# Attention with soft mixture of experts: the last 64 keys on four quarters of the array, and other positions in the order of tasks

## The chip, the cores and the metric

One core of one Trainium2 chip. The metric is device time of one execution in microseconds (us), the median of several runs; lower is better. The engines are TensorE (PE, its weight loads shown as PEld), VectorE (DVE), ScalarE (ACT), GpSimd (POOL) and SyncE (SP), which issues nearly all DMAs.

## The reference

Two stages. First attention over 8 batches, 8 heads, 576 positions and 64 dimensions, with rotary embedding; then a soft mixture of 8 experts with 4 slots each on its output.

```
q_rot, k_rot = rotate(q), rotate(k)
scores = (1 / sqrt(64)) * q_rot @ k_rot.T
attn = exp(scores - max(scores)); attn /= sum(attn) + 1e-9
x = (attn @ v), heads side by side: 4608 x 512
logits = x @ phi                        # 4608 x 32
d = softmax of logits over the rows;  slot_input = d.T @ x
slot_out = relu(slot_input @ w1[e]) @ w2[e]   # per expert
c = softmax of logits over the slots; out = c @ slot_out
```

## The kernel before

The work goes by pairs of heads: 32 pairs (4 per batch), two heads of a pair on the two halves of the 128 partitions. The 576 keys of a head are four blocks of 128 and a rest of 64; the 576 queries are two halves (n = 0, 1) of 288 columns. For one pair p the tasks are:

- load0, load1 (`fetch`, L136): q and k come in by SP into one of two buffers `x_in`. spin0, spin1 (L141, GpSimd) multiply by cosines and sines, join (L145, VectorE) adds the two parts, high0, high1 (L150, ScalarE) round to 16-bit halves, low (L154, VectorE) forms the remainders; it is the last reader of `x_in`, so it frees the buffer for the load of the pair after next.
- m00 to m31, m_rem (L172, L180, TensorE): 16-bit scores with the queries on the partitions; VectorE takes their maxima (L174, L182), m_min joins them (L186), m_turn, m_half and m_rows bring them as a row into `peak`.
- t00 to t31 (`t_unit`, L228): the scores with keys on the partitions, key block j, half n. Each is four products of 64 rows (high x high, high x low, low x high, and a product that subtracts the maximum) for two heads, which stand on the two row halves of the array and write the two banks of a PSUM buffer. ScalarE takes the exponential (L213) into `a_t`.
- t_rem (L215 to L220): the same for the last 64 keys. Head h reads row half h and writes partitions 64h to 64h + 63, for half n in bank n; first all of n = 0, then all of n = 1. ScalarE's exponential goes to `a_rem` (L220).
- av00 to av41 (L239): the product with v, accumulated in `o_ps` over five steps j. For j = 0 to 3, 128 keys on the rows and 64 columns per head; for j = 4, all 128 rows of `a_rem` (both heads) with a block of v that holds zeros for the other head. o_out (L246, ScalarE) copies the result out; there is one `o_ps`.
- add1, add2, add3 (L255, L257, VectorE) add up the exponentials over the key blocks, total (L269) sums them over the partitions with a matrix of ones and zeros, `pick`, total_out (L274, ScalarE) copies, send (L279 to L281, three DMAs on SP) lays the sums out as `rc`, recip (L287, L288, VectorE) forms 1 / sum, spread (L294) and widen (L301) are DMAs that broadcast it, norm (L304, GpSimd) applies it.
- logits and natural (L353 to L356, L339, L340) feed the second stage. Once per batch, stats hands a list of statistics to step0 to step3, which each work off one entry.

All engines' orders are written out by hand. The table `WHEN` gives each task a position: the fraction modulo 4 is its place in a cycle ("beat"), the quotient says how many pairs ahead or behind it runs. In each of the 32 beats the tasks run through in the order of these places, and each engine's queue follows from it. A beat of TensorE before the change is

```
t00 t01 m20 m21 | av30 av31 av40 av41 | t10 m30 | av00 | t11 m31 | av01 |
m_rem | total | t20 | m_turn | m01 t21 | av10 av11 | logits | t30 m10 m00 |
av20 | t31 m11 | natural | av21 | t_rem
```

where a bar stands where the form of the matmuls (rows x columns of the array that they use) changes. In the same beat VectorE's queue has m20, add3, m21, step0, m30, m31, m_rem, m_min, low, step1, m01, add1, logits_sum, stats, m10, m00, step2, m11, recip, add2, join, step3. SP's queue has widen, load0, load1, send, m_rows, weights, load_v, spread. All scores and small products take their turn in three PSUM buffers `s_ps` of two banks (`bank2`). After the last pair follow the statistics' end, the experts' two layers and the combination.

Of the kernel before, what the change touches and what calls it, by code (L numbers as in the profile page):

```python
# [7 lines left out]
F32 = mybir.dt.float32  # L8
# [7 lines left out]
B, H, S, D = 8, 8, 576, 64  # L16
HALF = D // 2
NP = H // 2
NPAIR = B * NP
DM = H * D  # L20
E, SPE, FF = 8, 4, 1024
NS = E * SPE
# [4 lines left out]
HC = S // 2  # L27
# [16 lines left out]
RC = 12  # L44
PIECE = 4
WHEN = {
    "load0": -15.85, "load1": -15.171, "spin0": -11.45, "spin1": -10.42, "join": -8.349, "high1": -7.786,
    "high0": -6.702, "low": -6.38, "m01": -5.7, "m10": -4.9, "m00": -4.892, "m11": -4.7, "m20": -3.754, "m21": -3.7,
    "m30": -2.9, "m31": -2.7, "m_rem": -2.531, "m_min": -2.49, "m_turn": -1.75, "m_half": -1.74, "m_rows": -1.541,
# [4 lines left out]
    "total_out": 5.55, "send": 5.56, "recip": 7.3, "spread": 7.31, "widen": 8.05, "norm": 9.3, "logits": 10.54,  # L54
    "logits_sum": 10.579, "stats": 10.6, "natural": 11.52, "natural_out": 11.536,
    "sums_turn": 6.0, "sums_wide": 6.3, "norm_wide": 6.4, "logits_late": 7.0, "logits_sum_late": 7.05,
    "natural_late": 7.3, "natural_out_late": 7.35,
    "trickle0": 0.55, "trickle1": 1.55, "trickle2": 2.55, "trickle3": 3.55,
}
QL, QH, KH, KL = range(4)  # L60

# [2 lines left out]
def attn_softmoe(ctx, tc, qk, v, phi, w1, w2, cs, ident, sel, seg, out):  # L64
    nc = tc.nc
    P = 128

    const = ctx.enter_context(tc.tile_pool(name="const", bufs=1))
# [21 lines left out]
    rows = (slice(0, 64), slice(64, P))  # L90
# [11 lines left out]
    peaks = [const.tile([P, S], F16, name=f"peak{i}") for i in range(2)]  # L102
    for t in peaks:
        nc.vector.memset(t, 0.0)
    pick = const.tile([P, 2, NS], F32, name="pick")
    nc.gpsimd.memset(pick, 0.0)
    nc.gpsimd.memset(pick[:, 0, 0:1], 1.0)
    for h in range(2):
        nc.gpsimd.memset(pick[rows[h], 1, h:h + 1], 1.0)

    nc.vector.memset(tiny, 0.0)
    nc.vector.memset(tiny[0:64], 1e-9)
# [14 lines left out]
    half = (slice(0, HC), slice(HC, S))  # L127
# [36 lines left out]
    def bank2():  # L164
        return ps_s.tile([P, 2, 512], F32, name="s_ps")
# [39 lines left out]
    ats = {}  # L205
    rems = {}
# [8 lines left out]
    def t_rem(p):  # L215
        rems[p] = att.tile([P, S], F32, name="a_rem")
        s = bank2()
        for n in range(2):
            score(p, s, slice(512, S), [(rows[h], h, n) for h in range(2)], lambda h, n: n)
        nc.scalar.activation(out=rems[p].rearrange("p (n x) -> p n x", n=2), in_=s[:, :, 0:HC], func=AF.Exp, scale=SCALE)  # L220

    def score(p, s, keys, outs, at):
        hl, pk = halves[p], peaks[p % 2]
        for i, (k, q) in enumerate(((KH, QH), (KH, QL), (KL, QH), (None, None))):
            for o, h, n in outs:
                lhs = lift[rows[h], 0:keys.stop - keys.start] if k is None else hl[rows[h], k, keys]
                rhs = pk[rows[h], half[n]] if k is None else hl[rows[h], q, half[n]]
                nc.tensor.matmul(s[o, at(h, n), 0:HC], lhsT=lhs, rhs=rhs, start=(i == 0), stop=(i == 3))  # L228
# [3 lines left out]
    def av(p, j, n):  # L232
        if j == 0 and n == 0:
            os_[p] = ps_o.tile([P, 2, 512], F32, name="o_ps")
        o, vt = os_[p], vts[p]
        for h in range(2):
            at = P * j + 64 * h
            rhs = ats[p, j][:, h, half[n]] if j < 4 else rems[p][:, half[n]]
            nc.tensor.matmul(o[rows[h], n, 0:HC], lhsT=vt[:, at:at + 64], rhs=rhs, start=(j == 0), stop=(j == 4))  # L239

    xts = {}
    xns = {}
# [21 lines left out]
    def total(p):  # L264
        c, r, a = cts.pop(p), rems[p], ats[p, 3]
        sg[p] = s = bank2()
        for n in range(2):
            for i, (k, m) in enumerate(((0, c[:, 0, half[n]]), (0, c[:, 1, half[n]]), (1, r[:, half[n]]), (0, a[:, 0, half[n]]))):
                nc.tensor.matmul(s[32 * i:32 * i + 32, n, 0:HC], lhsT=pick[:, k, :], rhs=m, start=True, stop=True,  # L269
                                 tile_position=(0, 32 * i))  # L270

    def total_out(p):
# [272 lines left out]
    def fast(task):  # L545
# [15 lines left out]
        "m_half": m_half,  # L561
        "m_rows": lambda p: m_rows(p, nc.sync),
        "t_rem": t_rem,
        "o_out": o_out,
        "add1": lambda p: add(p, 1),
        "add2": lambda p: add(p, 2),
        "add3": lambda p: add(p, 3),
        "total": total,
        "total_out": total_out,
        "send": slow(lambda p: send(p, nc.sync)),  # L570
# [24 lines left out]
    for j in range(5):  # L595
        for n in range(2):
            plan[f"av{j}{n}"] = lambda p, j=j, n=n: av(p, j, n)
# [10 lines left out]
    for t, cc in ((1, 0), (1, 1), (0, 0), (0, 1)):  # L608
        c = half[cc]
# [12 lines left out]
    o = bank2()  # L622
# [53 lines left out]
    p = NPAIR - 1  # L676
# [32 lines left out]
    m, al, dt, xn = state["m"], state["al"], state["dt"], xns.pop(B - 1)  # L709
# [27 lines left out]
    for i in range(NP):  # L737
        nc.tensor.matmul(rp[32 * i:32 * i + 32], lhsT=dn[0:64, P + 32 * i:P + 32 * i + 32],
                         rhs=xn[0:64, 4, i * P:(i + 1) * P], start=True, stop=True, tile_position=(0, 32 * i))
# [37 lines left out]
    def ffn1(grp, f):  # L777
        hp = ps_s.tile([P, 2, 512], F32, name="s_ps")
        for i in range(NP):
            for x in range(4):  # L780
                nc.tensor.matmul(hp[32 * x:32 * x + 32, 0, :], lhsT=st[:, i, SPE * (4 * grp + x):SPE * (4 * grp + x) + 32],  # L781
                                 rhs=w_tiles[16 * grp + 8 * f + 4 * (i // 2) + x][:, i % 2, :],
                                 start=(i == 0), stop=(i == NP - 1), tile_position=(0, 32 * x))
        hs = tail.tile([P, 512], F32, name="hs", bufs=2)
        nc.vector.tensor_scalar_max(out=hs, in0=hp[:, 0, :], scalar1=0.0)
        return hs
# [72 lines left out]
    for grp, f in ((0, 1), (1, 0), (1, 1)):  # L859
        h = ffn1(grp, f)  # L860
# [84 lines left out]
```

## Time and profile before

| | |
|---|---|
| median of 3 runs | 660.27 us (660.04 to 661.91) |
| the profiled execution | 662.53 us, span of its records 660.7 us |
| busy in that span | TensorE 603.1, VectorE 491.5, ScalarE 329.9, GpSimd 309.0 us |
| mean granted TensorE clock | 0.965 of full speed |
| moved by DMA | 102.58 MB |

The profile lists one execution. In a timeline a row gives the start in us, the length, the engine, the line (L228 is line 228 of the kernel), the operation, output <- inputs, and shapes; for matmuls "64*128" is rows x columns of the array. Brackets give idle time of the engine just before, and what ended it. Ends of matmuls are modelled and include the way through the array, so the pace is read from start to start.

### The profile page before, as it was taken

Reading aid. Unit: us, or ns where it says so; the run is one execution under the profiler, and the core shown is the slowest. Engines: PE = TensorE matmul, PEld = TensorE weight load, DVE = VectorE, ACT = ScalarE, POOL = GpSimd, SP = SyncE. Lnnn points to the kernel's source line nnn. Section 1 sums busy time; section 2 is a strip of 40 time slices with the busy share of each in tenths; the row PEclk is TensorE's granted clock in tenths of the full one; section 3 lists DMA queues with packets and bytes.
Section 4 is the critical chain, followed back from the end, with each engine's and each line's share of the span. In section 5 each row is a group of like instructions: output and inputs, shape, how many; then the busy total and the mean of one; then the engine's idle time right before and its main releaser. Section 6 shows DMA issues by size and latency. Waiting matters only on the chain.

```text
span 660.7 us, 15956 instructions
## 1 busy us (share of the span) xinstructions
PE 603.1 (91%) x6480; PEld 311.4 (47%) x6480; DVE 491.5 (74%) x729; ACT 329.9 (50%) x647; POOL 309.0 (47%) x310
## 2 busy tenths in 40 slices
PE   3699999999999999999999999999999999989981
PEld 2344444445444454444444544445444445543550
DVE  5787888898888788887889888988898773332251
ACT  1245555555555556455555555555555545323441
POOL 3683665565565565555635765546556200010000
PEclk9689999999999999999999999999999999859995
DMA  6143444444344444343434443434434135449997
GB/s 233 65 146 111 144 144 143 139 139 147 133 147 140 144 144 144 124 143 133 145 119 142 140 142 120 136 126 142 134 142 144 40 104 172 148 146 321 350 374 261
DMA packets 67746, 102.58 MB, mean 155 GB/s; under 512 B 16216, under 2 KB 43608, under 8 KB 67672
## 3 DMA queue, kind: packets, MB, share of 16 engines
q1 hardware_dynamic: 67658, 101.55, 46.4%
q8 instruction: 51, 0.84, 0.5%
q14 instruction: 23, 0.19, 0.1%
q10 hardware_dynamic: 14, 0.00, 0.0%
HBM read 91.54 MB, written 9.58 MB: 153 GB/s over the span
## 4 chain that ended last, share of the span: by engine, by line
PE 60%; ACT 13%; DVE 11%; issue 7%; DMA 6%; SPq 1%; ACTq 0%; DVEq 0%
PE o_ps L239 23%; PE s_ps L228 16%; ACT a_t L213 6%; DVE nm L174 6%; PE s_ps L172 3%; DMA rc<-s 3%; ACT s L274 3%; PE s_ps L781 2%; PE s_ps L339 2%; PE s_ps L269 2%; PE s_ps L180 2%; ACT a_rem L220 2%; PE s_ps L353 2%; DVE hl L154 1%; DMA w_exp<-in_w 1%
## 5 line engine op out<-in xcount | busy, mean ns | idle before, releaser
L141 POOL TENSOR_TENSOR x_in<-x_in,cs_sb 128x288 f32<-128x288 f32 x248 | 259.1, 1076 | 43.3 <-DMA x_in<-in_qk 41.4
L213 ACT ACTIVATE a_t<-s_ps 128x576 f32<-128x576 f32 x256 | 162.8, 648 | 132.3 <-PE s_ps L228 131.9
L174 DVE TENSOR_REDUCE nm<-s_ps 128x2 f32<-128x576 f32 x256 | 188.4, 753 | 33.3 <-PE s_ps L172 31.5
L228 PE MATMUL s_ps<-hl 64*128 64x288 f16 (+1 forms) x1920 | 171.5, 286 | 8.6 <-ACT a_t L213 7.9
L239 PE MATMUL o_ps<-a_t,v_in 128*64 128x288 f32 x1024 | 168.1, 428 | 1.0 <-ACT xt L246 0.3
L304 POOL TENSOR_TENSOR xt<-xt,rb 128x576 f32<-128x576 f32 x30 | 43.4, 1446 | 198.7 <-DMA rb<-r_row 149.9
L228 PEld LDWEIGHTS <-hl 64*128 64x128 f16 (+1 forms) x1920 | 79.3, 96 | 106.1 <-issue 91.1
L228 PE MATMUL s_ps<-peak,lift 64*128 64x288 f16 (+1 forms) x640 | 92.7, 284 | 0.0
L172 PE MATMUL s_ps<-hl 64*128 64x288 f16 x512 | 70.0, 287 | 16.0 <-DVE nm L174 7.3
L239 PEld LDWEIGHTS o_ps<-a_t,v_in 128*64 128x64 f32 x1024 | 56.7, 136 | 55.5 <-issue 30.0
L150 ACT CAST hl<-x_in 128x576 f16<-128x576 f32 (+1 forms) x66 | 43.1, 654 | 38.9 <-DVE x_in L145 36.7
L154 DVE TENSOR_TENSOR hl<-x_in,hl 128x1152 f16<-128x1152 f32 x32 | 52.6, 1643 | 0.5 <-ACT hl L150 0.5
L172 PEld LDWEIGHTS <-hl 64*128 64x128 f16 x512 | 31.8, 94 | 33.6 <-issue 22.6
L255 DVE TENSOR_TENSOR c_t<-a_t 128x1152 f32<-128x1152 f32 x32 | 47.3, 1480 | 0.2 <-PE s_ps L269 0.2
L145 DVE TENSOR_TENSOR x_in<-x_in 128x1152 f32<-128x1152 f32 (+2 forms) x36 | 47.3, 1313 | 0.2
L255 DVE TENSOR_TENSOR c_t<-c_t,a_t 128x1152 f32<-128x1152 f32 x32 | 45.4, 1419 | 0.0
L274 ACT ACTIVATE s<-s_ps,bits 128x576 f32<-128x576 f32 x32 | 23.7, 740 | 34.7 <-issue 24.1
L269 PE MATMUL s_ps<-c_t,pick 128*32 128x288 f32 x256 | 37.3, 412 | 0.0
L269 PE MATMUL s_ps<-a_rem,pick 128*32 128x288 f32 x128 | 37.0, 412 | 0.0
L269 PE MATMUL s_ps<-a_t,pick 128*32 128x288 f32 x128 | 37.0, 412 | 0.0
L239 PE MATMUL o_ps<-a_rem,v_in 128*64 128x288 f32 x256 | 36.5, 406 | 0.0
L228 PEld LDWEIGHTS <-lift 64*128 64x128 f16 (+1 forms) x640 | 33.0, 97 | 7.0 <-issue 0.4
(186 smaller groups left out, 587.7 us busy)
## 6 DMA issues: line engine op xcount, KB each, us to landing
x_in<-in_qk SPq DMA_DIRECT2D x62, 576.0 KB
w_exp<-in_w SPq DMA_DIRECT2D x63, 512.0 KB
v_in<-in_v SPq DMA_DIRECT2D x32, 320.0 KB
rb<-r_row SPq DMA_DIRECT2D x60, 144.0 KB
out<-w_exp SPq DMA_DIRECT2D x16, 512.0 KB
x_in<-in_qk SPq DMA_DIRECT2D x4, 288.0 KB
out<-w_exp SPq DMA_DIRECT2D x4, 256.0 KB
rc<-s SPq DMA_DIRECT2D x60, 4.5 KB
```

The source lines that it names most:

```text
L141: eng.tensor_tensor(out=x[:, :, c], in0=x[:, :, c], in1=cs_sb[:, :, c], op=ALU.mult)
L145: nc.vector.tensor_tensor(out=x[:, t, 0, c], in0=x[:, t, 0, c], in1=x[:, t, 1, c], op=ALU.add)
L154: nc.vector.tensor_tensor(out=hl[:, 0:4:3], in0=x[:, :, 0], in1=hl[:, 1:3], op=ALU.subtract)
L172: nc.tensor.matmul(s[:, h, 0:HC], lhsT=hl[rows[h], QH, P * j:P * j + P], rhs=hl[rows[h], KH, half[n]], start=True, stop=True)
L174: nc.vector.tensor_reduce(out=nms[p][:, n, j:8:4], in_=s[:, :, 0:HC], axis=AX.X, op=ALU.max, negate=True)
L213: nc.scalar.activation(out=ats[p, j][:, :, half[n]], in_=s[:, :, 0:HC], func=AF.Exp, scale=SCALE)
L228: nc.tensor.matmul(s[o, at(h, n), 0:HC], lhsT=lhs, rhs=rhs, start=(i == 0), stop=(i == 3))
L239: nc.tensor.matmul(o[rows[h], n, 0:HC], lhsT=vt[:, at:at + 64], rhs=rhs, start=(j == 0), stop=(j == 4))
L255: nc.vector.tensor_tensor(out=c, in0=c if j > 1 else ats[p, 0], in1=a, op=ALU.add)
L269: nc.tensor.matmul(s[32 * i:32 * i + 32, n, 0:HC], lhsT=pick[:, k, :], rhs=m, start=True, stop=True, tile_position=(0, 32 * i))
L274: nc.scalar.activation(out=s4.rearrange("p (n x) -> p n x", n=2), in_=s[:, :, 0:HC], func=AF.Identity, bias=tiny)
L304: eng.tensor_tensor(out=xts[p], in0=xts[p], in1=rbs.pop(p), op=ALU.mult)
```

## The change

t_rem goes through both halves of the queries in one sweep, and for the second half the heads change places: head h still reads row half h, but writes partitions of half 1 - h. Four matmuls that follow one another then stand on four different quarters (64 rows x 64 columns) of the array. The product with v for j = 4 reads only the 64 rows of `a_rem` that belong to its head, against a block of v that holds both heads' last values instead of zeros; it too uses the four quarters, two per half n. `pick` gets one more column, so that total finds the heads in their new places.

In `WHEN`, 15 tasks get another position. In the queues this gives: on TensorE, m21 goes from behind m20 to behind av41, t21 from ahead of av10 to behind av11, and av21 from behind natural to directly behind av20; on VectorE, join goes from ahead of step3 to behind it; on SP, load_v goes ahead of weights. spin0 and norm get other numbers, and GpSimd's cyclic order of norm, spin1, spin0 stays.

```diff
-    "load0": -15.85, "load1": -15.171, "spin0": -11.45, "spin1": -10.42, "join": -8.349, "high1": -7.786,
+    "load0": -15.902, "load1": -15.171, "spin0": -13.817, "spin1": -10.42, "join": -7.985, "high1": -7.786,
...
-    "high0": -6.702, "low": -6.38, "m01": -5.7, "m10": -4.9, "m00": -4.892, "m11": -4.7, "m20": -3.754, "m21": -3.7,
+    "high0": -6.702, "low": -6.38, "m01": -5.7, "m10": -4.9, "m00": -4.892, "m11": -4.7, "m20": -3.771, "m21": -3.317,
...
-    "load_v": -1.2, "t00": 0.0, "t01": 0.2, "step0": 0.7, "t10": 1.0, "av00": 1.159, "t11": 1.2, "av01": 1.448,
-    "step1": 1.7, "t20": 2.0, "t21": 2.315, "add1": 2.39, "av10": 2.5, "av11": 2.504, "weights": 2.737, "t30": 3.0,
-    "step2": 3.146, "av20": 3.163, "t31": 3.2, "add2": 3.54, "av21": 3.565, "t_rem": 3.612, "step3": 3.666,
+    "load_v": -1.419, "t00": 0.0, "t01": 0.2, "trickle0": 0.55, "step0": 0.7, "t10": 1.024, "av00": 1.159, "t11": 1.2,
+    "av01": 1.448, "trickle1": 1.55, "step1": 1.7, "t20": 2.032, "add1": 2.39, "av10": 2.5, "av11": 2.504,
+    "t21": 2.511, "trickle2": 2.55, "weights": 2.626, "t30": 3.0, "step2": 3.146, "av20": 3.163, "av21": 3.179,
+    "t31": 3.2, "add2": 3.469, "trickle3": 3.55, "t_rem": 3.612, "step3": 3.666, "add3": 4.295, "av30": 4.5,
...
-    pick = const.tile([P, 2, NS], F32, name="pick")
+    pick = const.tile([P, 2 * NS + 1], F32, name="pick")
     nc.gpsimd.memset(pick, 0.0)
-    nc.gpsimd.memset(pick[:, 0, 0:1], 1.0)
-    for h in range(2):
-        nc.gpsimd.memset(pick[rows[h], 1, h:h + 1], 1.0)
+    nc.gpsimd.memset(pick[:, 0:1], 1.0)
+    for h in (0, 1, 2):
+        nc.gpsimd.memset(pick[rows[h % 2], NS + h:NS + h + 1], 1.0)
...
-        for n in range(2):
-            score(p, s, slice(512, S), [(rows[h], h, n) for h in range(2)], lambda h, n: n)
+        score(p, s, slice(512, S), [(rows[h ^ n], h, n) for n in range(2) for h in range(2)], lambda h, n: n)
...
-            at = P * j + 64 * h
-            rhs = ats[p, j][:, h, half[n]] if j < 4 else rems[p][:, half[n]]
-            nc.tensor.matmul(o[rows[h], n, 0:HC], lhsT=vt[:, at:at + 64], rhs=rhs, start=(j == 0), stop=(j == 4))
+            at = P * j + 64 * (h if j < 4 else n)
+            r = slice(0, P) if j < 4 else rows[h ^ n]
+            rhs = ats[p, j][:, h, half[n]] if j < 4 else rems[p][r, half[n]]
+            nc.tensor.matmul(o[rows[h], n, 0:HC], lhsT=vt[r, at:at + 64], rhs=rhs, start=(j == 0), stop=(j == 4))
...
-            for i, (k, m) in enumerate(((0, c[:, 0, half[n]]), (0, c[:, 1, half[n]]), (1, r[:, half[n]]), (0, a[:, 0, half[n]]))):
-                nc.tensor.matmul(s[32 * i:32 * i + 32, n, 0:HC], lhsT=pick[:, k, :], rhs=m, start=True, stop=True,
+            for i, (k, m) in enumerate(((0, c[:, 0, half[n]]), (0, c[:, 1, half[n]]), (NS + n, r[:, half[n]]),
+                                        (0, a[:, 0, half[n]]))):
+                nc.tensor.matmul(s[32 * i:32 * i + 32, n, 0:HC], lhsT=pick[:, k:k + NS], rhs=m, start=True, stop=True,
...
-    vt = np.zeros((NPAIR, 2, 64, 2, D), np.float32)
-    for h in range(2):
-        vt[:, h, :, h] = vr[:, h, 512:]
+    vt = np.stack([vr[:, :, 512:], vr[:, ::-1, 512:]], axis=3)
```

More of the change, by code (lines that the diff above doesn't have):

```diff
@@ L46 @@
 WHEN = {
-    "load0": -15.85, "load1": -15.171, "spin0": -11.45, "spin1": -10.42, "join": -8.349, "high1": -7.786,
-    "high0": -6.702, "low": -6.38, "m01": -5.7, "m10": -4.9, "m00": -4.892, "m11": -4.7, "m20": -3.754, "m21": -3.7,
-    "m30": -2.9, "m31": -2.7, "m_rem": -2.531, "m_min": -2.49, "m_turn": -1.75, "m_half": -1.74, "m_rows": -1.541,
[4 rows of a table removed]
[L54 to L58, printed above, removed]
+    "load0": -15.902, "load1": -15.171, "spin0": -13.817, "spin1": -10.42, "join": -7.985, "high1": -7.786,
+    "high0": -6.702, "low": -6.38, "m01": -5.7, "m10": -4.9, "m00": -4.892, "m11": -4.7, "m20": -3.771, "m21": -3.317,
+    "m30": -2.9, "m31": -2.7, "m_rem": -2.531, "m_min": -2.49, "m_turn": -1.75, "m_half": -1.667, "m_rows": -1.541,
[4 rows of a table added]
+    "av31": 4.504, "av40": 4.51, "av41": 4.514, "o_out": 4.52, "total": 5.54, "total_out": 5.55, "send": 5.56,
+    "sums_turn": 6.0, "sums_wide": 6.3, "norm_wide": 6.4, "logits_late": 7.0, "logits_sum_late": 7.05, "recip": 7.3,
+    "natural_late": 7.3, "spread": 7.31, "natural_out_late": 7.35, "widen": 8.05, "norm": 9.093, "logits": 10.54,
+    "logits_sum": 10.579, "stats": 10.716, "natural": 11.52, "natural_out": 11.536,
 }
```

1 row of the table WHEN is left out of this document.

## The prediction

> **What bounds the kernel now.** I read the page first (shares, slices, chain), then TensorE's timeline through one task cycle ("beat"), then the tables of waits and VectorE's timeline through the same beat.
>
> ```profile
> PE 603.1 (91%) x6480; PEld 311.4 (47%) x6480; DVE 491.5 (74%) x729; ACT 329.9 (50%) x647; POOL 309.0 (47%) x310
> ...
> PE 60%; ACT 13%; DVE 11%; issue 7%; DMA 6%; SPq 1%; ACTq 0%; DVEq 0%
> ```
>
> TensorE is busy nine tenths of the time and carries 60% of the chain that ended last. But VectorE, ScalarE and DMA make up another 30% of that chain, so there is a second candidate. The length of a beat comes from the exponential of the last 64 keys, which runs once per pair of heads:
>
> ```profile
> L220 ACT ACTIVATE a_rem<-s_ps x32: 650/650/654, 44.2 to 572.3; 128x576 f32<-128x576 f32 x32
> ```
>
> 31 beats in 528.1 us are 17.04 us each. TensorE's timeline (start, length of the merged piece, instruction, count, and in brackets a real idle time):
>
> ```profile
> 299.93 1.14 PE L239 MATMUL o_ps<-a_rem,v_in 128*64 128x288 f32 x8
> ...
> 304.16 0.44 PE L269 MATMUL s_ps<-c_t,pick 128*32 128x288 f32 x2
> 304.17 0.43 PE L269 MATMUL s_ps<-a_rem,pick 128*32 128x288 f32 x1
> 304.18 0.43 PE L269 MATMUL s_ps<-a_t,pick 128*32 128x288 f32 x1
> 304.43 0.41 PE L269 MATMUL s_ps<-c_t,pick 128*32 128x288 f32 x2
> ...
> 306.25 0.30 PE L172 MATMUL s_ps<-hl 64*128 64x288 f16 x2
> 306.79 0.54 PE L228 MATMUL s_ps<-hl 64*128 64x288 f16 x6 [0.24 <-ACT a_t L213]
> ...
> 307.38 1.19 PE L239 MATMUL o_ps<-a_t,v_in 128*64 128x288 f32 x8
> 308.50 0.43 PE L353 MATMUL s_ps<-xt,phi_sb 128*32 128x128 f32 x8
> ...
> 311.98 0.71 PE L239 MATMUL o_ps<-a_t,v_in 128*64 128x288 f32 x4
> 312.61 0.56 PE L228 MATMUL s_ps<-hl 64*64 64x288 f16 x6
> 313.00 0.29 PE L228 MATMUL s_ps<-peak,lift 64*64 64x288 f16 x2
> ...
> 313.71 0.54 PE L228 MATMUL s_ps<-hl 64*128 64x288 f16 x6
> ...
> 314.70 0.29 PE L172 MATMUL s_ps<-hl 64*128 64x288 f16 x2
> 315.17 0.30 PE L172 MATMUL s_ps<-hl 64*128 64x288 f16 x2 [0.18 <-ACT a_t L213]
> 315.40 1.19 PE L239 MATMUL o_ps<-a_t,v_in 128*64 128x288 f32 x8
> 316.42 1.14 PE L239 MATMUL o_ps<-a_rem,v_in 128*64 128x288 f32 x8
> 317.49 0.30 PE L228 MATMUL s_ps<-hl 64*128 64x288 f16 x2
> ```
>
> From 299.93 to 316.42, the same task in two neighbouring beats, this beat took 16.49 us; the mean is 0.55 higher, because one batch in four beats adds its statistics. Pieces' lengths include a pipeline tail, so I count from start to start. Matmuls go abreast when they use different parts of the array: at 304.16 to 304.18 four stand side by side on four column strips and the next four follow at 304.43; at 313.00 two are through in 0.29 us, on the two quarters of the diagonal. The two bracketed waits (306.79, 315.17) are for ScalarE to empty a PSUM buffer.
>
> The second candidate shows in the waits of VectorE and of the SP queue, and in VectorE's timeline:
>
> ```profile
> DVE rr L287 <- DMA rc<-s: 26.5, 23, 2.0
> ```
> ```profile
> SPq L136 <- DVE hl L154: 186.2, 29, 14.9
> ```
> ```profile
> 313.72 0.19 DVE L287 TENSOR_REDUCE rr<-rc 96x12 f32<-96x36 f32 x1 [1.68 <-DMA rc<-s]
> ...
> 318.38 1.42 DVE L174 TENSOR_REDUCE nm<-s_ps 128x2 f32<-128x576 f32 x2
> 320.01 0.76 DVE L174 TENSOR_REDUCE nm<-s_ps 128x2 f32<-128x576 f32 x1 [0.21 <-PE s_ps L172]
> 321.01 0.76 DVE L182 TENSOR_REDUCE nm<-s_ps 128x2 f32<-128x576 f32 x1 [0.24 <-PE s_ps L180]
> ...
> 321.89 1.68 DVE L154 TENSOR_TENSOR hl<-x_in,hl 128x1152 f16<-128x1152 f32 x1
> ...
> 329.93 0.19 DVE L287 TENSOR_REDUCE rr<-rc 96x12 f32<-96x36 f32 x1 [0.80 <-DMA rc<-s]
> ```
>
> This is a ring. VectorE adds up the sums (`recip`, L287), and behind that in its queue stand add2, join, the maxima and `low` (L154), which ends at 323.57. `low` frees the input buffer that SP's next load waits for (29 waits, 186 us), and `send` is queued on SP behind that load; its DMA `rc` is what the next `recip` waits for, 23 times in 30. From recip to low's end is 9.85 us, from there to the next recip 6.36: once round takes 16.21 us, beside TensorE's 16.49. Both bound this kernel almost equally; TensorE is just ahead.
>
> **The change, part by part.** On TensorE, per beat:
>
> t_rem. Its 16 matmuls take from 312.61 to 313.71, 1.10 us, two abreast in eight steps. A step is 0.124 us (from 313.71 to 314.70 there are 16 matmuls of 288 columns, two abreast). On four quarters they need four steps: minus 0.49. Fewer is excluded, since each quarter gets four in sequence. Four quarters at once, two in each row half and two in each column half, is a form that the trace does not show. Its ends are four abreast, as with the column strips of L269, and single file, 16 x 0.124 = 1.98 us, or 0.99 more than now. I take four abreast: rows show two row halves abreast (313.71, 64*128) and four column strips with different moving data abreast (304.16), and the quarters only combine them.
>
> The product with the last keys (L239 on a_rem). A group of eight records costs 1.12 with its start and the change to the next array form (307.38 to 308.50), one of four costs 0.63 (311.98 to 312.61), so a step is 0.245. Now av30 to av41 take 1.02 + 1.07 = 2.09 (315.40 to 317.49). Afterwards the first eight end in a change of form (1.12) and the four-quarter group takes two steps, 0.63: 1.75, minus 0.34. In single file it would be eight steps in place of two, 1.47 more than that.
>
> m21 behind av41. m20 and m21 take 0.70 (314.70 to 315.40), most of it the wait. Alone, m20 costs 0.23 (315.17 to 315.40), and m21 costs 0.12 ahead of t10, which has its form: minus 0.35. ScalarE is done with the buffer by then, 1.7 us later.
>
> t21 behind av10/av11. m01 and t21 take 1.13 (306.25 to 307.38). Alone m01 costs 0.23 and t21 0.59 (306.79 to 307.38): minus 0.31, the wait gone. t21's exponential comes later on ScalarE, and t30's behind it, but half of ScalarE's time is free. av21, which reads it, still comes after logits, t30, m10 and m00.
>
> av21 directly behind av20: two groups of 0.63 become one of 1.12, minus 0.14.
>
> Sum: 0.49 + 0.34 + 0.35 + 0.31 + 0.14 = 1.63 us per beat; TensorE alone would need 14.86 in an ordinary beat and 15.41 in the mean.
>
> The rest costs nothing that I can find. GpSimd keeps its cyclic order (norm, spin1, spin0); only the number of the pair in the table changes. join passes step3, which is empty in two beats of four and short in the others. On SP, load_v goes ahead of the weights: v arrives earlier, and a weight issue later that is wanted only after attention. `total` keeps shape and count, with one more column in pick.
>
> The ring. None of these steps is taken out of it: order and sizes from recip to low, SP's load ahead of send, and the DMA all stay. With TensorE at 14.86, the ring's 16.21 decides. In that turn VectorE waited 0.21 and 0.24 for TensorE. These may stay, since the matmuls waited for need a buffer that VectorE itself has just emptied, or go: 15.76 to 16.21. I take the middle, 16.0. The batch's statistics add 0.55 to the mean now; some stand in the ring (updates on VectorE), some are TensorE's alone. Between 0 and 0.55 I take 0.35: 16.35 per beat against 17.04, minus 0.69. So TensorE gains 1.63 and waits most of it away, for VectorE's reductions that empty its PSUM buffers.
>
> Over the run: about 27 beats at 0.69 are 18.6 us. The last four beats have no load ahead of send, so the ring is shorter there and TensorE's gain comes through; with fewer max units in two of them I count 1.4 each, 5.6. The last pair's t_rem and product lie behind the beats: 0.8. Together 25.0. The profiled execution took 662.5 us (span 660.7, 1.8 around it) and would take 637.5; it stood 2.3 above the median of 660.3, so the median goes to **635 us**.
>
> **The rivals.**
>
> TensorE stays the bound because the ring gives way (rc landing earlier, say). All 1.63 come through: 31 x 1.63 + 0.8 = 51, so 609 us. For it: the ring's 6.36 includes a DMA time that could shrink. Against: the loads issued just ahead of rc stay. 0.07.
>
> The quarters run only two abreast. TensorE's mean is then 15.41 + 0.83 = 16.24, still under the ring's 16.35; only the last four beats and the last pair lose 0.8 each: 639 us. Against it are the rows named under t_rem; for it, that no row has this form. 0.12.
> The Trainium skill, page "TensorEngine Tiling (Array Packing)", section Restrictions and Gotchas, says "Different row tiles cannot access same PSUM bank simultaneously"; in the change the two heads of one half of the queries lie on different row halves and write one bank, so by that rule they would not run together, and the time would be this rival's. The trace disagrees already before the change: the two at 313.00 are such a pair, in one bank, and take 0.29 us together.
>
> The ring is longer than I read it: at 16.75 per beat (rc landing later behind the loads, or VectorE's additions slower beside GpSimd) only 0.29 x 27 + 6.4 = 14 are saved: 646 us. For it: single turns scatter, since one wait before recip is 1.68 and the next 0.80. 0.14.
>
> Slower: the quarters go in single file, because two matmuls in one row half or one column half block each other. TensorE then needs 1.48 more in t_rem and 1.47 more in the product than I counted: 15.41 + 2.95 = 18.36 per beat against 17.04, plus 1.32 x 31 = 41, so 701 us. It turns slower as soon as these two groups cost 1.63 more than counted. Against it: column strips and row halves each run abreast in the rows above. 0.07.
>
> The change does not reach the end of the chain (within 0.3%, 2 us, about what a measurement here can tell from nothing): only if the ring already stood at 17.04 in the mean. 0.04.
>
> **How the numbers follow.** The forecast keeps 0.56, for 626 to 642 by its ends (ring 16.0 plus or minus 0.2 on 27 beats, and the share of the statistics). Leaving out 609, no change and slower leaves out 0.18; the range from 618 to 650 holds the rest, with 618 for a ring that gives way by half. Faster: 0.56 + 0.07 + 0.12 + 0.14 = 0.89; same 0.04; slower 0.07.
>
> **What would show it.** t_rem from its first matmul to t00 in about 0.61 us with 16 records of form 64*64; the a_rem group in 64*64 with eight records in about 0.63; the two waits for ScalarE at L172 and L228 gone. If the ring binds, starts of L287 lie 15.8 to 16.2 apart in ordinary beats, VectorE's waits for rc remain, and TensorE shows gaps ended by VectorE's L174, ahead of t11 above all. Wrong would be: pairs of 64*64 still 0.12 apart two by two (quarters not abreast), no gaps on TensorE with beats near 15 (no ring), or turns of the ring over 16.5.

## The result, and the profile after

The changed kernel takes **643.93 us**, the median of four runs (640.89 to 645.37), against 660.15 us for the kernel before on the same chip (four runs, 658.49 to 661.91). The ratio is 0.9748, with a 95% interval of 0.9705 to 0.9791, so 16.2 us are saved where 25 were forecast. The profiled execution took 640.89 us, the lowest of its four, with a span of 639.1. Times here and below leave out a run that lies over 1.5% above the fastest of its kernel; that is one run, of the changed kernel with a longer ring.

The page of the changed kernel, busy time and then the shares of the chain that ended last:

```profile
PE 572.4 (90%) x6480; PEld 293.6 (46%) x6480; DVE 493.2 (77%) x729; ACT 324.1 (51%) x647; POOL 315.0 (49%) x311
...
PE 35%; DVE 31%; DMA 13%; issue 8%; SPq 6%; ACT 4%; DVEq 0%; ACTq 0%
```

TensorE has lost 31 us of busy time and its share of the chain fell from 60% to 35%. VectorE went from 11% to 31%, DMA from 6% to 13%, and SP's queue from 1% to 6%: three members of the ring. Line numbers moved by one or two: t_unit's scores are now at L226, the maxima at L173, m_rem at L179, the product with v at L238, join at L144, low at L153, the loads at L135; recip stays at L287.

TensorE's timeline of the changed kernel, over what the prediction priced:

```profile
288.32 0.56 PE L226 MATMUL s_ps<-hl 64*64 64x288 f16 x12
288.71 0.29 PE L226 MATMUL s_ps<-peak,lift 64*64 64x288 f16 x4
288.93 0.54 PE L226 MATMUL s_ps<-hl 64*128 64x288 f16 x6
...
290.14 1.19 PE L238 MATMUL o_ps<-a_t,v_in 128*64 128x288 f32 x8
291.26 0.71 PE L238 MATMUL o_ps<-a_rem,v_in 64*64 64x288 f32 x8
291.91 0.30 PE L171 MATMUL s_ps<-hl 64*128 64x288 f16 x2
...
293.29 0.30 PE L171 MATMUL s_ps<-hl 64*128 64x288 f16 x2 [0.59 <-DVE nm L173]
...
310.14 0.30 PE L171 MATMUL s_ps<-hl 64*128 64x288 f16 x2 [1.51 <-DVE nm L173]
```

t_rem takes 0.61 us from its first matmul to t00 (288.32 to 288.93), as forecast: 16 matmuls in four steps. The product with the last keys takes 0.65 (291.26 to 291.91), forecast 0.63. So four quarters do run abreast. The new gaps of 0.59 and 1.51 us stand ahead of m30 (L171 at 293.29 and 310.14): it needs a PSUM buffer that VectorE's maximum of m20 has to empty.

The table of waits of the changed kernel (waiter, what it waited for: us in total, times, longest):

```profile
DVE rr L287 <- DMA rc<-s: 23.4, 24, 1.5
...
PE s_ps L171 <- DVE nm L173: 19.3, 29, 1.8
```

In the kernel before, TensorE waited in this way 8 times for 7.3 us; now it is 29 times for 19.3. Of the two waits for ScalarE's `a_t`, 30 times each before, one of 0.3 us is left. A small wait is new: the product with v waits for o_out, ScalarE's copy that empties `o_ps` (L245), 22 times for 5.9 us in all.

The chain in order of time through one turn (start, length, what), short pieces and the second load's issue left out:

```profile
289.00 0.20 DVE rr L287
...
289.37 1.32 DVE c_t L254
...
290.75 1.74 issue
292.49 0.75 DVE nm L173
293.24 0.66 DVE c_t L256
293.90 0.68 DVE nm L173
...
294.62 0.67 PE s_ps L226 x8
295.29 0.12 PE s_ps L171 x2
295.41 0.64 PE o_ps L238 x4
296.05 0.38 PE s_ps L179 x4
...
296.45 0.77 DVE nm L181
...
297.43 1.27 DVE hl L153
...
298.75 0.33 SPq L135
...
299.65 0.58 SPq L279
300.28 0.70 SPq L280
...
301.03 4.61 DMA rc<-s
...
305.77 0.20 DVE rr L287
```

This is the ring of the prediction, link by link: recip, add2, join (the "issue" at 290.75 lies inside join's 1.95 us), maxima, low, the two loads, the three issues of send, the landing of `rc`, recip. It goes through TensorE for 1.8 us (294.62 to 296.43), the place of VectorE's two small waits.

### The profile page after: what moved, and what is told of

The parts are those of the page before. It is cut to its first block, busy times and chain, and to the rows that moved or that the text cites. A ratio compares the mean times of both kernels' runs of the same rounds, so it can differ in the third digit from the quotient of the medians.

```text
span 639.1 us, 15934 instructions
## 1 busy us (share of the span) xinstructions
PE 572.4 (90%) x6480; PEld 293.6 (46%) x6480; DVE 493.2 (77%) x729; ACT 324.1 (51%) x647; POOL 315.0 (49%) x311
## 4 chain that ended last, share of the span: by engine, by line
PE 35%; DVE 31%; DMA 13%; issue 8%; SPq 6%; ACT 4%; DVEq 0%; ACTq 0%
DMA rc<-s 10%; PE o_ps L238 10%; DVE nm L173 10%; PE s_ps L226 8%; DVE c_t L254 6%; DVE hl L153 5%; DVE c_t L256 3%; PE s_ps L171 2%; PE s_ps L781 2%; DVE nm L181 2%; SPq L280 2%; SPq L135 2%; PE s_ps L179 2%; SPq L279 2%; DVE x_in L144 2%
## 5 line engine op out<-in xcount | busy, mean ns | idle before, releaser
L140 POOL TENSOR_TENSOR x_in<-x_in,cs_sb 128x288 f32<-128x288 f32 x248 | 264.2, 1098 | 36.9 <-DMA x_in<-in_qk 24.7
L173 DVE TENSOR_REDUCE nm<-s_ps 128x2 f32<-128x576 f32 x256 | 187.2, 752 | 30.9 <-PE s_ps L171 29.8
L238 PE MATMUL o_ps<-a_t,v_in 128*64 128x288 f32 x1024 | 160.1, 423 | 5.9 <-ACT xt L245 5.9
L226 PE MATMUL s_ps<-hl 64*128 64x288 f16 (+1 forms) x1920 | 156.0, 287 | 4.1 <-DVE nm L173 1.6
L226 PEld LDWEIGHTS <-hl 64*128 64x128 f16 (+1 forms) x1920 | 71.8, 96 | 89.3 <-issue 73.2
L171 PE MATMUL s_ps<-hl 64*128 64x288 f16 x512 | 72.8, 288 | 23.9 <-DVE nm L173 19.3
L238 PEld LDWEIGHTS o_ps<-a_t,v_in 128*64 128x64 f32 x1024 | 59.4, 136 | 55.9 <-issue 18.3
L226 PE MATMUL s_ps<-peak,lift 64*128 64x288 f16 (+1 forms) x640 | 83.8, 284 | 1.1 <-DMA peak<-mr 1.1
L171 PEld LDWEIGHTS <-hl 64*128 64x128 f16 x512 | 32.4, 94 | 55.0 <-issue 45.1
L153 DVE TENSOR_TENSOR hl<-x_in,hl 128x1152 f16<-128x1152 f32 x32 | 55.2, 1725 | 0.5 <-ACT hl L149 0.5
L144 DVE TENSOR_TENSOR x_in<-x_in 128x1152 f32<-128x1152 f32 (+2 forms) x36 | 48.5, 1347 | 0.2
L226 PEld LDWEIGHTS <-lift 64*128 64x128 f16 (+1 forms) x640 | 30.1, 97 | 7.6 <-issue 1.5
L181 DVE TENSOR_REDUCE nm<-s_ps 128x2 f32<-128x576 f32 x32 | 24.2, 758 | 6.9 <-PE s_ps L179 6.8
```

Of the source, the lines that this page charges most:

```text
L140: eng.tensor_tensor(out=x[:, :, c], in0=x[:, :, c], in1=cs_sb[:, :, c], op=ALU.mult)
L144: nc.vector.tensor_tensor(out=x[:, t, 0, c], in0=x[:, t, 0, c], in1=x[:, t, 1, c], op=ALU.add)
L153: nc.vector.tensor_tensor(out=hl[:, 0:4:3], in0=x[:, :, 0], in1=hl[:, 1:3], op=ALU.subtract)
L171: nc.tensor.matmul(s[:, h, 0:HC], lhsT=hl[rows[h], QH, P * j:P * j + P], rhs=hl[rows[h], KH, half[n]], start=True, stop=True)
L173: nc.vector.tensor_reduce(out=nms[p][:, n, j:8:4], in_=s[:, :, 0:HC], axis=AX.X, op=ALU.max, negate=True)
L238: nc.tensor.matmul(o[rows[h], n, 0:HC], lhsT=vt[r, at:at + 64], rhs=rhs, start=(j == 0), stop=(j == 4))
```

## The experiments

The theory: the change takes TensorE off the limit, and what is left is the ring's turn. The rivals: TensorE still sets the beat and gained less than its rows say; or the ring was the bound already before, and the other new positions made the gain. Ratios are to the kernel before on the same chip.

**The two halves of the change.** First the new table alone on the code before, then the new code with the old table.

```diff
 WHEN = {
-  (the table before)
+  (the table after)            # e1_order: code before
                                # e2_quarters: code after, table before
```

> The new table of positions alone, with the last 64 keys as before (two quarters at a time). TensorE's own work per beat falls by 0.80 us (m21 0.35, t21 0.31, av21 0.14), from 17.04 to 16.24 in the mean, still a little under the ring's 16.5 that the changed kernel shows. Ring theory (VectorE, SP and the DMA of the sums set the beat once TensorE is faster): almost the whole gain is there already; only the last four beats and the last pair lack the quarters, about 4 us: 646 to 650 us. Sharing theory (each part brings its own share of TensorE's saving, and some general loss takes the rest): 0.80 of 1.63, so half of the 16 us: 652 us. TensorE theory (TensorE alone sets the beat): 660 - 25 = 635 us.

> The four quarters alone (t_rem, product with v, pick), with the table of positions as before. TensorE's own work falls by 0.83 us per beat, to 16.21 in the mean; its two waits for ScalarE stay. Ring theory: most of the 16 us is there again, 645 to 650 us, so that the gains of both halves alone add up to clearly more than the whole. Sharing theory: 652 us, the halves add up to the whole. TensorE theory: 660 - 26 = 634 us. In the profile t_rem should take 0.61 us and the a_rem group 0.63 as in the changed kernel.

The order alone: 647.79 us, ratio 0.9823 (0.9764 to 0.9881). The quarters alone: 648.36 us, 0.9847 (0.98 to 0.9894). Each half is worth 1.8% and 1.5%, together 3.3%, while both at once give 2.5%. That the parts add up to more than the whole is what a second limit gives, but the intervals are too wide to rest on it. What they do exclude is TensorE alone, which would have given 634 to 635 us for either half. With the quarters alone TensorE keeps its 30 waits for ScalarE at t21, as it should.

**Send ahead of the loads**, in both kernels. The loads get a position just behind send on SP, so send no longer stands behind a load that waits for low.

```diff
-    "load0": -15.902, "load1": -15.171,
+    "load0": -14.434, "load1": -14.432,      # on the kernel before: from -15.85, -15.171
```

> The changed kernel with load0 and load1 moved behind send in SP's queue (positions -14.434 and -14.432), so that send does not wait for low and rc is not queued behind 1.2 MB of loads. Ring theory: from total_out's end to rc's landing it takes about 2 us of issue and 2 to 3 us of DMA, so recip comes 1.5 to 3 us earlier, the ring falls under TensorE's 15.4, and TensorE binds again: 644 - 27 x 0.9 to 1.1 = 614 to 620 us, and TensorE's idle time ended by VectorE's L173 (19.3 us in all) goes. If the ring is not what binds (TensorE's own waits, PSUM buffers, VectorE's throughput), nothing moves by more than 3 us: 641 to 647; if the later loads starve GpSimd and VectorE instead, slower than 644.

> The kernel before with the same move of load0 and load1 behind send. Ring theory as in the prediction: before the change TensorE was just ahead of the ring, so shortening the ring brings only the beats in which a late rc pushed through (16.62 to 16.74 against 16.49): 655 to 660 us. If the ring already set the beat before the change, it brings about as much as in the changed kernel, 640 us or less.

This separates the theories best. On the kernel before: 661.70 us, ratio 1.0035 (1.0007 to 1.0063), so cutting the ring there gains nothing, where up to 5 us had been expected. The edit does cut it: recip no longer waits for `rc` at all (23 waits, 26.5 us before), and yet 21 of its first 27 beats last 16.49, 16.62 or 18.45 us (to 0.02), where the kernel before has 22 such beats. On the changed kernel: **631.39 us**, 0.9568 (0.9513 to 0.9624), 12.5 us below the changed kernel's median; the intervals of the two ratios do not touch. The ring bounds the kernel after and did not bound the kernel before. In the latter VectorE only waits longer for TensorE, 49.8 us where it was 31.5:

```profile
DVE nm L174 <- PE s_ps L172: 49.8, 90, 3.3
```

The size was missed: 614 to 620 had been expected of the changed kernel. Its VectorE timeline without the ring (two stretches):

```profile
292.88 2.47 DVE L153 TENSOR_TENSOR hl<-x_in,hl 128x1152 f16<-128x1152 f32 x1
...
299.78 0.76 DVE L173 TENSOR_REDUCE nm<-s_ps 128x2 f32<-128x576 f32 x1 [0.90 <-PE s_ps L171]
300.46 0.18 DVE L287 TENSOR_REDUCE rr<-rc 96x12 f32<-96x36 f32 x1
```

recip has no bracket: it starts straight behind m11's maximum, though `rc` has landed. What sets the beat now? Its chain is TensorE's for one half again:

```profile
PE 50%; DVE 21%; DMA 10%; issue 8%; ACT 5%; SPq 2%; POOL 2%; DVEq 0%; ACTq 0%; POOLq 0%
```

The windows from 100 to 400 us (length, then busy time of TensorE, its weight loads, VectorE, ScalarE, GpSimd), first of the changed kernel, then with send first:

```profile
100.00:400.00 300.00, 281.61 (x3311) 142.70 (x3312) 264.34 (x375) 167.47 (x340) 183.81 (x169) 1.00 0.43 142
```
```profile
100.00:400.00 300.00, 286.81 (x3409) 145.18 (x3407) 273.62 (x385) 172.30 (x347) 229.84 (x173) 1.00 0.43 149
```

TensorE is busy 286.8 of the 300 us and VectorE 273.6, both more than in the changed kernel, and no single limit is left. Two beats without statistics take only 14.70 us, with TensorE idle for 0.1, which bears out the 14.86 that were forecast for TensorE alone; but the mean of the first 27 beats is 16.24. In six of the seven with statistics TensorE is idle for 0.3 us at most and so the limit again; in the other 20 it idles for 1.0 in the mean, behind `peak`, the maxima and others. Why just these waits remain is not shown. GpSimd is busy 46 us longer: its products take 1.40 us in the mean, where they took 1.11, and 102 us of them lie beside VectorE's additions, where it was 64. A new wait of TensorE is of another kind:

```profile
PE s_ps L226 <- DMA peak<-mr: 8.3, 10, 1.6
```

The row of maxima, `peak`, is issued behind the loads and now comes late for TensorE. Two more kernels take that apart, the first with the loads behind m_rows too, the second with only load1 behind send.

```diff
-    "load0": -15.902, "load1": -15.171, "spin0": -13.817,
+    "load0": -13.535, "load1": -13.533, "spin0": -13.5,      # e5_send_rows_first
+    "load0": -15.902, "load1": -14.432, "spin0": -13.817,    # e10_one_load_behind_send
```

> The changed kernel with load0, load1 behind both send and m_rows in SP's queue (positions -13.535, -13.533; spin0 to -13.5, which leaves GpSimd's order as it is). In the kernel with the loads behind send alone (631 us) TensorE waited 8.3 us for peak, the row of maxima, which had got behind the loads. If that is what now ends last there, it goes, and the time falls to 622 to 628 us. If VectorE's own queue ends last there, 629 to 633 us. If the loads come too late for GpSimd and VectorE, 634 us or more, with VectorE waiting for GpSimd's products ahead of join.

> The changed kernel with load1 alone behind send on SP; load0 stays ahead, so send still waits for low, but rc has only half the loaded bytes ahead of it. If the ring's DMA part is the queueing of rc behind the loads (3.8 us from the third issue to landing, against 2.1 with both loads behind), about half of that goes: 0.4 us of issue and 0.8 us of queueing, 1.2 of the 1.0 to 1.5 us per beat that matter: 630 to 637 us. If what counts is that send waits for low, most of the 644 us stays: 639 to 645.

With the rows first too: 629.51 us, ratio 0.9517 (0.9459 to 0.9575). The wait for `peak` is gone and the time hardly moves against 631.39, within both intervals. Another wait has come in its place: GpSimd's norm is late, and TensorE waits for it five times, 7.0 us in all. With load0 still ahead of send: 633.02 us, 0.9557 (0.9519 to 0.9594). send still waits there behind a load that waits for low, yet nearly all of the gain is kept, and recip waits for `rc` only once in the run, for 0.6 us. The trace's records of the semaphores say why: between 100 and 500 us, `rc` lands 3.7 us in the mean after its third issue in the changed kernel (3.8 in the kernel before), where both loads, 1.2 MB, go ahead of it; 2.8 us with one load ahead of it, and 2.1 us with none (the first of these runs). With the second load's 0.42 us of issue on SP, that takes about 1.3 us out of the turn, and that is enough for recip to wait no longer.

**A longer ring**, in both kernels: one more small DMA ahead of send's three, whose result nobody reads.

```diff
+        eng.dma_start(out=junk, in_=s4[0:64:32])
         eng.dma_start(out=rc[:, 0, :], in_=s4[0:64:32])
```

> The changed kernel with one more small DMA ahead of send's three on SP (4.5 KB of the same sums into a tile that nobody reads): it lies between low and rc, so it lengthens the ring by one issue, about 0.6 us, and nothing else. Ring theory: nearly all of it shows in each of some 26 beats, plus 12 to 16 us: 656 to 660 us. If the ring does not set the beat, nothing moves: 641 to 647 us.

> The kernel before with the same additional DMA in the ring. Ring theory: there TensorE was just ahead, and recip started 0.6 us ahead of the end of the beat in the mean, so only the late beats pay: plus 2 to 7 us, 662 to 667 us. If the ring had set the beat before the change as well, plus 12 to 16 us: 672 to 676 us.

On the changed kernel 653.17 us, ratio 0.9855 (0.9787 to 0.9922); on the kernel before 668.01 us, 1.0125 (1.0064 to 1.0185). Against their own bases that is 1.1% and 1.25%: the two do not separate, the first is under the 12 us that were expected at least, and the second is 1 us over its range. The edit was a poor one for the question. send started 0.6 us later, but the time from the third issue of `rc` to recip shrank from 4.0 to 3.7, because `rc` lands only behind the loads anyhow. And in the kernel before, a ring of 16.21 and 0.6 more passes TensorE's 16.49, so both had to lose.

**More work on TensorE**, in both kernels: the first half of t10 is computed twice into the same buffer, 0.49 us per beat.

```diff
-        score(p, s, slice(P * j, P * j + P), ...)
+        for _ in range(2 if (j, n) == (1, 0) else 1):
+            score(p, s, slice(P * j, P * j + P), ...)
```

> The changed kernel with the first half of t10 computed twice into the same buffer (eight more matmuls, 0.49 us of TensorE per beat, same result), just ahead of m30, where TensorE waits for VectorE. Ring theory: TensorE has time to spare there, so it is mostly absorbed: plus 1 to 6 us, 645 to 650 us. If TensorE set the beat in the changed kernel: plus 15, 659 us.

> The kernel before with the same eight more matmuls. Theory of the prediction: TensorE is just ahead of the ring there, so most of 0.49 x 31 = 15 us shows: 669 to 676 us. If the ring already set the beat before the change: 661 to 666 us.

On the changed kernel 650.01 us, ratio 0.9816 (0.9746 to 0.9885); on the kernel before 670.52 us, 1.0126 (1.0084 to 1.0168). Of 15 us added, about 4.5 come through in the first (0.7%, and the intervals reach nothing) and 8.5 in the second. The direction is the theory's, but the two intervals overlap. The profiles don't separate them either: the first 27 beats grow from 16.49 to 16.90 us in the mean in the first (an execution of 653.56 us, one of the two longer of its four) and from 16.96 to 17.38 in the second. This pair leaves the question open. In the second, ScalarE's exponential of the last keys waits for TensorE each time and comes at regular steps (in this kernel it stands at L221, the scores at L229):

```profile
302.37 0.65 ACT L221 ACTIVATE a_rem<-s_ps 128x576 f32<-128x576 f32 x1 [1.06 <-PE s_ps L229]
319.26 0.65 ACT L221 ACTIVATE a_rem<-s_ps 128x576 f32<-128x576 f32 x1 [1.06 <-PE s_ps L229]
```

That beat takes 16.89 us, 0.40 above the 16.49 in the kernel before, so most of the 0.49 arrives when TensorE sets the beat.

**t_rem in another order.** The four products of one quarter directly behind one another, then the next quarter, in place of four quarters in turn.

```diff
-        score(p, s, slice(512, S), [(rows[h ^ n], h, n) for n in range(2) for h in range(2)], lambda h, n: n)
+        for n in range(2):
+            for h in range(2):
+                score(p, s, slice(512, S), [(rows[h ^ n], h, n)], lambda h, n: n)
```

> The changed kernel with t_rem's 16 matmuls in another order: all four of one quarter, then all four of the next, same operands and results. If matmuls start in the order of the queue, t_rem goes in single file, up to 16 x 0.124 = 1.98 us in place of 0.49 and its start, so TensorE needs about 1.3 to 1.5 us more per beat, 16.7 to 16.9 against the ring's 16.5: 648 to 656 us, less than the 41 us that 1.3 per beat would be without the ring. If TensorE finds the free quarters by itself, t_rem stays at 0.6 us and the time at 641 to 647 us.

646.20 us, ratio 0.979 (0.9746 to 0.9833), which overlaps with the change's 0.9705 to 0.9791. Its TensorE timeline (the scores are at L228 here):

```profile
291.58 0.59 PE L228 MATMUL s_ps<-hl 64*64 64x288 f16 x12
291.98 0.32 PE L228 MATMUL s_ps<-peak,lift 64*64 64x288 f16 x4
292.23 0.54 PE L228 MATMUL s_ps<-hl 64*128 64x288 f16 x6
```

t_rem takes 0.65 us here too. The queue holds three products from `hl`, one from `lift`, four times over, but the first of `lift` starts 0.40 us after the start, near the end, with the other three. The order is not that of the changed kernel either: the first four start 13 to 14 ns apart here, 3 to 4 ns there. The run had been meant to slow t_rem; it says instead that TensorE starts matmuls of a free quarter ahead of those queued for a busy one.

**The other moves alone**: the new table again, but m21, t21 and av21 at their old places, on the code before.

```diff
-    ... "m21": -3.317, ... "t21": 2.511, ... "av21": 3.179,
+    ... "m21": -3.7, ... "t21": 2.315, ... "av21": 3.565,
```

> The kernel before with all the other new positions, but m21, t21 and av21 left where they were: TensorE's queue is that of before; join goes behind step3, load_v ahead of weights, the rest only changes numbers. The prediction costed these at nothing: 658 to 662 us. If v's earlier load or join's place is worth something, 3 us or more below 660; if they cost, above 663.

658.53 us, ratio 0.9954 (0.9929 to 0.9978): a gain of 1.5 to 4.7 us from moves that the prediction costed at nothing. Its cause is open; beats are as long as before in the profiles (16.95 and 16.96 us), and what this execution gains lies ahead of the first exponential of the last keys, 2.3 us, and behind the last, 1.4. So these moves, worth 0.5%, do not make the 2.5% of the change.

## Why the prediction was right, and where its size was off

**The terms of TensorE held.** t_rem and the product came within 0.02 us, m21 stands at 0.13 (291.91 to the next group at 292.04 in the trace), and the waits for ScalarE at L172 and L228 went but for one. The quarters run abreast, so the rivals of two abreast and single file fall, and with them the rule of the Trainium skill, page "TensorEngine Tiling (Array Packing)", section Restrictions and Gotchas, on different row tiles and one bank: two heads of one half write one bank, and all four stand abreast.

**The change of the bound held.** The chain after is the ring, TensorE waits for VectorE's maxima, and cutting the ring pays 12.5 us after the change and nothing before it. The place of the gaps was named wrongly: they lie ahead of m30, not of t11. And single turns scatter more than the 15.8 to 16.2 us that were named as a sign: from the first recip to the 27th they run from 15.0 to 17.7, and 14 of 26 lie over the 16.5 that were to speak against the forecast; the mean is 16.5, with the statistics in it. In this stretch the starts of recip lie 16.77 and 16.16 us apart:

```profile
289.00 0.19 DVE L287 TENSOR_REDUCE rr<-rc 96x12 f32<-96x36 f32 x1 [0.51 <-DMA rc<-s]
...
290.62 1.95 DVE L144 TENSOR_TENSOR x_in<-x_in 128x1152 f32<-128x1152 f32 x1
...
295.45 0.76 DVE L173 TENSOR_REDUCE nm<-s_ps 128x2 f32<-128x576 f32 x1 [0.22 <-PE s_ps L171]
296.45 0.76 DVE L181 TENSOR_REDUCE nm<-s_ps 128x2 f32<-128x576 f32 x1 [0.24 <-PE s_ps L179]
...
305.77 0.19 DVE L287 TENSOR_REDUCE rr<-rc 96x12 f32<-96x36 f32 x1 [1.34 <-DMA rc<-s]
...
321.93 0.19 DVE L287 TENSOR_REDUCE rr<-rc 96x12 f32<-96x36 f32 x1 [0.69 <-DMA rc<-s]
```

**The step that failed is "I take the middle, 16.0", with the mean of 17.04 that it was set against.** The exponentials of the last keys tell how much. Before, the first, the 28th and the last:

```profile
44.19 0.65 ACT L220 ACTIVATE a_rem<-s_ps 128x576 f32<-128x576 f32 x1 [1.24 <-PE s_ps L228]
...
502.18 0.65 ACT L220 ACTIVATE a_rem<-s_ps 128x576 f32<-128x576 f32 x1 [1.06 <-PE s_ps L228]
...
572.28 0.65 ACT L220 ACTIVATE a_rem<-s_ps 128x576 f32<-128x576 f32 x1 [0.96 <-PE s_ps L228]
```

and after:

```profile
42.76 0.65 ACT L218 ACTIVATE a_rem<-s_ps 128x576 f32<-128x576 f32 x1
...
487.91 0.65 ACT L218 ACTIVATE a_rem<-s_ps 128x576 f32<-128x576 f32 x1
504.38 0.65 ACT L218 ACTIVATE a_rem<-s_ps 128x576 f32<-128x576 f32 x1
519.73 0.65 ACT L218 ACTIVATE a_rem<-s_ps 128x576 f32<-128x576 f32 x1
535.88 0.65 ACT L218 ACTIVATE a_rem<-s_ps 128x576 f32<-128x576 f32 x1
554.91 0.66 ACT L218 ACTIVATE a_rem<-s_ps 128x576 f32<-128x576 f32 x1
```

- The first 27 beats: 457.99 us before, 16.96 each, and 445.15 after, 16.49 each. That saves 0.47 per beat, 12.8 us, where 0.69 and 18.6 were forecast. 0.08 of the missing 0.22 is the base: 17.04 is the mean of all 31 beats, and the last four are longer (17.5). The other 0.14 is the turn: 16.49 in place of 16.35. Split by beat, the 20 without statistics take 16.25 in the mean, 0.25 more than the 16.0 that was taken, and the seven with statistics 17.17, so that their share in the mean is 0.24, 0.11 less than the 0.35 that was taken. So the upper end of the ring, 16.21, was right for an ordinary turn. VectorE's two waits for TensorE, 0.22 and 0.24, stayed in this turn, and over the run its waits for the maxima's matmuls are 36.6 us, where they were 39.5. The argument for it stood in the prediction (the matmuls need a buffer that VectorE itself has just emptied), and the middle was taken all the same.
- The last four beats: 70.10 before, 67.00 after, 3.1 saved where 5.6 were forecast. The first of them still takes 16.47 (487.91 to 504.38), because its recip waits for an `rc` sent behind a load of the beat before, so it saves nothing; the other three save 1.1, 1.2 and 0.7.
- What was not in the sum: the first beat starts 1.4 us earlier, and the work behind the last exponential takes 84.1 us (639.1 less 554.9) where it took 88.4 in the execution before. In ten of the twelve experiments it takes 86.9 to 88.0, in two 81.0 and 82.2, whichever code they have; nothing in the change touches it beyond the 0.8 of the last pair. With the beats above these are the 21.6 us between the two spans. So the profiled execution, at 640.9, flatters the change by about 3 us, and the four runs' median is the figure to keep.

**The rival of a longer ring** (646 us, at 16.75 per beat) was near in time and partly right in cause: turns do scatter, and VectorE's additions are longer beside GpSimd. low over the whole run (min, median, max in ns), before and then after:

```profile
L154 DVE TENSOR_TENSOR hl<-x_in,hl x32: 1346/1509/2521, 12.6 to 526.4; 128x1152 f16<-128x1152 f32 x32
```
```profile
L153 DVE TENSOR_TENSOR hl<-x_in,hl x32: 1348/1664/2499, 11.6 to 511.4; 128x1152 f16<-128x1152 f32 x32
```

Its median rose by 0.16 us. The landing of `rc`, though, takes as long as before (3.8 us in the mean, now 3.7), so the part "rc landing later behind the loads" did not happen.

**"The rest costs nothing"** was right in sign for the path and wrong by a little: those moves are worth 1.5 to 4.7 us, on the good side.

## What to carry to other kernels

When two limits lie within a few per cent of each other, a gain on one is worth only the distance to the other, so price the second limit's turn as carefully as the change, and take a wait that the text itself explains at its full length. Follow a ring through every queue on it: here a small DMA stood behind two large loads, and one number in the table (load1 behind send) gave about 11 us more. Cutting a ring in the kernel before, where it gains nothing, is the cheapest proof that the limit has moved.

## What the runs showed of the hardware

Matmuls on four different quarters run four abreast: 16 of 64 rows x 288 columns take 0.61 us. Of the four at a time, the two that write one bank stand on different row halves and write different partitions.

They do so even when queued one quarter at a time (0.65 us). The Trainium skill, page "TensorE: Matmul & The Clock Gate", section "The mechanism", says that matmuls go in strict order, with no reordering. The run with t_rem quarter by quarter disagrees: in strict order a quarter's second product would hold up the other quarters, and with two abreast only where one quarter's last product meets the next one's first, 16 matmuls of 0.124 us take 13 steps, 1.6 us.

A sum or difference over 1152 columns on VectorE takes 1.34 us by the median of join and up to 1.95 beside GpSimd's products (2.5 for low), while the maxima, which read PSUM, keep 0.74 to 0.76 us beside them. The Trainium skill, page "SBUF — State Buffer", section "Who interferes with whom", states that a VectorE instruction with two SBUF inputs contends with a GpSimd instruction that reads SBUF; these rows agree. GpSimd is the one that loses more: in the changed kernel its product of 288 columns takes 0.79 us by the median when clear of such additions, and 1.91 when more than half of it lies beside one.

A DMA of 2.2 KB issued behind two loads of 576 KB on the same queue landed 3.7 us after its issue in the mean, behind one load 2.8 us, and ahead of both 2.1 us.
